# Another table of moved works in the plan of a causal attention and a two-layer product

## The chip, the cores and the metric

One Trainium2 chip, one core of it. The metric is the device time of one execution in microseconds; three executions give a median. A profiled execution is a run of its own, with its own time.

## The reference, cut to what matters

Four batches of twelve heads attend over 448 positions of 64 elements; the result, 1792 tokens of 768 elements, goes through two matrix products with an ELU between them. Everything is float32, except that the two weight matrices arrive as float64.

```python
scores = scale * np.matmul(q, k.transpose(0, 1, 3, 2))      # 4 x 12 x 448 x 448
scores = np.where(np.triu(ones, k=1), -1e9, scores)
attn = np.exp(scores - np.max(scores, axis=-1, keepdims=True))
attn = attn / (np.sum(attn, axis=-1, keepdims=True) + 1e-09)
x = np.matmul(attn, v)          # transposed and reshaped to 1792 x 768
h = x @ w_in                    # 768 x 2048
g = np.where(h > 0.0, h, np.exp(np.minimum(h, 0.0)) - 1.0)
return (g @ w_out)              # 2048 x 768
```

## The kernel before

**The work.** Positions are cut into four chunks of 112. Heads go in pairs (six of them), one head on each half of the 128 partitions. The first chunk of each pair is done first (`first_pair`, its q, k and v loaded at L500 and L505), then the second (`attention(False)`), then the third and fourth together (`attention(True)`, "joint"). Of a unit of attention TensorE (PE) makes the scores `sc` (L614, first chunk L515); VectorE (DVE) adds the mask and takes the row minimum of the negated scores `nm` (`softmax`, L419); ScalarE (ACT) takes the exponential and the row sums (L423); PE transposes the result (`tr`, L679), an engine copies it to SBUF (`at`: L683 on ACT, L684 on DVE), and PE multiplies it with v (`av`, L647, first chunk L453).

**The precision.** A float32 product is made as three matmuls (`three`, L817 to L819) of a rounded high part and a low part of each factor. The high part is a cast (`hi_lo`: L775 on ACT, or L776 on DVE) and the low part a subtraction on DVE (L778). The tile `whl` holds both parts of a weight tile, `qkhl` those of a joint pair's q and k (loaded as `qk`), `xh` and `xl` those of x. The first scores and the first hidden tiles use plain float32 (L515, L840).

**The weights.** A tile of `w_in` comes as 64-bit words (`load64`, L728). `convert` turns it into float32 in a chain of five steps that alternates between two engines: L736 on DVE, L740 on ACT, L741 on DVE, L744 on ACT (needs only the words, so it may be done early), and L747 on DVE. The converted tile is also stored (`kin`) and fetched again for the later tokens (`w<-kin`). Tiles of `w_out` are converted in the same way in the background, and four additions or subtractions (`add`, L783) mix four tiles for the products of the joint half.

**The ELU.** ACT makes `m` from a finished bank `hp` in two steps (L913, L914), and DVE makes `G` from both (L915).

**What sets the order.** Nothing is ordered by hand. All work is declared as 3130 works to a `Plan`, each with the engine that may do it, a rough cost, what it reads and writes, and a due time that is worked back from the PE work that needs it. A work with two ways, such as the casts of `hi_lo` and the copies `at`, may go to either engine. `draft` is a list scheduler: it walks through a model of time, and on the engine that is free earliest it places, among the ready works that can start within 0.12 us of each other, the one that is wanted first. The instructions are then issued in that order, so each engine executes its own row of works strictly in order, and an instruction that has to wait holds up all that stands behind it. All 449 DMAs are issued by SyncE (SP) in its row. The table that the change replaces enters in one line: the number of a work (in order of declaration) gives the microseconds by which its wanted time is moved, forward where positive.

```python
w.want = w.due - shift.get(w.n, 0.0)      # L218; shift is Plan.SOONER
```

**The stages.** PE's long stretches are: the first chunk with the first hidden tiles (0 to 30 us), the second chunk with the first half of the hidden layer (to about 120 us), the joint attention between products of the two halves (to about 375 us), and from there products alone.

Of the kernel before, what the change touches and what calls it, by code (L numbers as in the profile page):

```python
# [108 lines left out]
class Plan:  # L109
# [21 lines left out]
    def add(self, ways, reads=(), writes=(), due=None, size=0.0, hold=(), after=None):  # L131
# [24 lines left out]
        return w  # L156

    SOONER = {
# [30 lines left out]
    }  # L189

    def rank(self):
# [1038 lines left out]
```

## Time and profile before

| | us |
|---|---|
| three executions | 602.19, 604.09, 604.17 (median 604.09) |
| profiled execution, its time | 602.11 |
| its span in the profile | 600.3 |
| PE busy in the span | 588.2 (98%) |
| DVE busy | 517.3 (86%) |
| ACT busy | 440.6 (73%) |
| granted TensorE clock | 0.999 of full speed |

The span is what the profiler sees from the first to the last instruction; 1.8 us of the execution's own time lie around it. An engine's busy time is counted without the instructions that only wait, branch or issue DMAs.

### The profile page before, as it was taken

To read this page: it belongs to the slowest core of one execution; us is meant where nothing else is said; L and a number is where in the kernel's file an instruction comes from. 1 tells how busy PE (TensorE), PEld (TensorE's weight loads), DVE (VectorE), ACT (ScalarE), POOL (GpSimd) and SP (SyncE) were. 2 spreads that over 40 slices of the span, in tenths; PEclk is the share of its full clock that TensorE was granted. 3 is DMA by queue.
4 is the path that set the end of the run, shared out by engine and by line. 5 is a ranking of instruction groups with operands and counts; after the bars stand their busy time and mean duration, and the time that the engine had idled before them with its cause. 6 is when DMAs were issued, how large, how long until landed. Compare 5 with 4: busy or idle time off the path is not lost.

```text
span 600.3 us, 11631 instructions
## 1 busy us (share of the span) xinstructions
PE 588.2 (98%) x4086; PEld 518.2 (86%) x4086; DVE 517.3 (86%) x1212; ACT 440.6 (73%) x980; POOL 1.5 (0%) x12
## 2 busy tenths in 40 slices
PE   6999999999999999999999999999999999999997
PEld 5766888888788888888888889999999999999996
DVE  4889999999999999998999897699878999998511
ACT  6999989899899989887779766258747886574300
POOL 0000000000000000000000000000000000000000
PEclk9999999999999999999999999999999999999999
DMA  9999999988999999875456588996953334451111
GB/s 228 250 346 342 374 287 316 279 240 252 327 325 298 348 318 280 278 214 169 139 166 199 156 288 256 334 329 238 319 159 106 106 105 132 117 141 53 46 48 46
DMA packets 113610, 134.36 MB, mean 224 GB/s; under 512 B 42512, under 2 KB 86800, under 8 KB 113552
## 3 DMA queue, kind: packets, MB, share of 16 engines
q1 hardware_dynamic: 113552, 133.62, 72.2%
q8 instruction: 32, 0.52, 0.4%
q14 instruction: 26, 0.21, 0.1%
HBM read 101.45 MB, written 32.15 MB: 223 GB/s over the span
## 4 chain that ended last, share of the span: by engine, by line
PE 91%; DMA 2%; ACT 2%; SPq 2%; DVE 2%; issue 0%; ACTq 0%
PE op L817 12%; PE op L819 11%; PE op L818 11%; PE hp L817 11%; PE hp L819 10%; PE hp L818 10%; PE av L647 6%; PE tr L679 6%; PE sc L614 6%; PE hp L840 3%; DMA v<-in_v 1%; DMA w<-kin 1%; SPq L500 1%; PE av L453 1%; SPq L505 1%; ACT a L423 1%
## 5 line engine op out<-in xcount | busy, mean ns | idle before, releaser
L775 ACT ACTIVATE whl<-w 128x768 fp32r<-128x768 f32 x102 | 85.4, 842 | 75.5 <-PE op L819 41.2
L817 PE MATMUL op<-ph,whl 128*128 128x448 f32 (+1 forms) x338 | 126.4, 374 | 0.0
L819 PE MATMUL op<-ph,whl 128*128 128x448 f32 (+1 forms) x338 | 123.1, 364 | 0.0
L818 PE MATMUL op<-pl,whl 128*128 128x448 f32 (+1 forms) x338 | 123.1, 364 | 0.0
L778 DVE TENSOR_TENSOR whl<-w,whl 128x768 fp32r<-128x768 f32 x108 | 102.4, 953 | 14.4 <-ACT whl L775 14.0
L423 ACT ACTIVATE a<-a,nm 112x336 f32<-112x336 f32 (+3 forms) x192 | 98.0, 522 | 11.9 <-DVE nm L419 11.7
L419 DVE CUSTOM_DVE_ANT_0 a<-sc,mask 112x336 f32<-112x336 f32 (+3 forms) x192 | 74.7, 443 | 9.3 <-PE sc L515 7.4
L817 PEld LDWEIGHTS op<-ph,whl 128*128 128x128 f32 x338 | 63.5, 188 | 8.8 <-issue 3.8
L819 PEld LDWEIGHTS op<-ph,whl 128*128 128x128 f32 x338 | 63.5, 188 | 5.2
L818 PEld LDWEIGHTS op<-pl,whl 128*128 128x128 f32 x338 | 63.6, 188 | 4.5
L817 PE MATMUL hp<-xh,whl 128*128 128x448 f32 x168 | 65.6, 390 | 0.0
L819 PE MATMUL hp<-xh,whl 128*128 128x448 f32 x168 | 61.4, 366 | 0.0
L818 PE MATMUL hp<-xl,whl 128*128 128x448 f32 x168 | 61.4, 366 | 0.0
L818 PE MATMUL hp<-pl,whl 128*128 128x448 f32 x168 | 61.4, 365 | 0.0
L817 PE MATMUL hp<-ph,whl 128*128 128x448 f32 x168 | 61.4, 365 | 0.0
L819 PE MATMUL hp<-ph,whl 128*128 128x448 f32 x168 | 61.3, 365 | 0.0
L679 PE MATMUL tr<-ident,a 112*112 112x112 f32 x432 | 50.2, 259 | 0.5 <-DVE nm L419 0.4
L679 PEld LDWEIGHTS tr<-ident,a 112*112 112x112 f32 x432 | 45.1, 133 | 5.8 <-DVE nm L419 1.1
L683 ACT ACTIVATE at<-tr 112x448 f32<-112x448 f32 (+1 forms) x109 | 47.5, 497 | 1.5 <-PE tr L679 1.5
L647 PEld LDWEIGHTS av<-at,v 112*64 112x64 f32 x864 | 41.5, 137 | 5.5 <-issue 3.1
L647 PE MATMUL av<-at,v 112*64 112x112 f32 x864 | 45.4, 261 | 0.0
L913 ACT ACTIVATE m<-hp 128x448 f32<-128x448 f32 x56 | 30.2, 538 | 13.9 <-DVE hp L908 7.0
(96 smaller groups left out, 990.4 us busy)
## 6 DMA issues: line engine op xcount, KB each, us to landing
w<-kin SPq DMA_DIRECT2D x40, 384.0 KB, 5.4
w<-in_w_in SPq DMA_DIRECT2D x16, 768.0 KB, 9.1
w<-in_w_out SPq DMA_DIRECT2D x24, 512.0 KB, 6.3
w<-sout SPq DMA_DIRECT2D x32, 384.0 KB, 3.4
w<-kout SPq DMA_DIRECT2D x24, 384.0 KB, 3.2
qk<-in_qk SPq DMA_DIRECT2D x24, 336.0 KB, 5.3
kin<-w SPq DMA_DIRECT2D x16, 384.0 KB, 7.1
sout<-w SPq DMA_DIRECT2D x12, 512.0 KB, 5.6
```

What stands on the lines that cost most here:

```text
L419: plan.add(dve(n, lambda: nc.vector.tensor_tensor_reduce(out=a()[:, c], in0=sc()[:, c], in1=mask[:, S - n:], op0=ALU.add, op1=ALU.min, sca ...
L423: plan.add(act(n, lambda: nc.scalar.activation(a()[:, c], a()[:, c], AF.Exp, bias=nm()[:, x:x + 1], scale=-1.0, accum_out=su()[:, x:x + 1] ...
L614: nc.tensor.matmul(sc[half]()[:, lo:lo + n], s["q"](d, x), s["k"](d, y, n), start=i == 0, stop=i == len(s["split"]) - 1,)
L647: nc.tensor.matmul(av()[half_of(half), chunk(u % 4)], o["v"][1](half, i), at()[:, chunk(x)], start=i == 0, stop=i == chunks(u) - 1,)
L679: nc.tensor.transpose(tr()[:, chunk(x)], a[:, chunk(i)], ident)
L683: act(w, lambda: nc.scalar.activation(at()[:, :w], tr()[:, :w], AF.Copy)),
L775: act(n, lambda: nc.scalar.activation(h(), x(), AF.Copy), 0.09),
L778: sub = lambda eng: lambda: eng.tensor_tensor(out=l(), in0=x(), in1=f32(h()), op=ALU.subtract)
L817: nc.tensor.matmul(acc(), wh(k), xh(), start=first, stop=False, skip_group_check=more)
L818: nc.tensor.matmul(acc(), wh(k), xl(), start=False, stop=False, skip_group_check=more)
L819: nc.tensor.matmul(acc(), wl(k), xh(), start=False, stop=last, skip_group_check=more)
L913: plan.add(act(S, lambda: nc.scalar.activation(m(), h(), AF.Relu, scale=-1.0)), [h], [m])
```

## The change

The dictionary `Plan.SOONER` is replaced by another one, of 232 entries for 278. No work is added, removed or changed; the lines behind the table stand five lower in the changed file (L747 becomes L742, and so on). The core of the diff:

```diff
     SOONER = {
-        0: 284.3, 1: 284.4, 7: -8.8, 12: 1.9, 14: -2.2, 15: -3.8, 17: 0.4, 21: -14.5, 23: -45.2, 31: 0.6,
...
-        954: -56.2, 957: 27.7, 958: 15.4, 963: 11.1, 966: -8.3, 968: 88.8, 977: 58.1, 978: 7.9, 982: -7.1,
...
+        0: 668.6, 1: 670, 3: -4.9, 14: -1.3, 15: -10.9, 19: 4.7, 21: -8.6, 23: -35.1, 32: -1.1, 33: -17.8,
...
+        916: 5.3, 932: 23.9, 952: -11.7, 954: -11.8, 957: 32.2, 964: 338.3, 965: -159.4, 968: 198.3, 972: 12.7,
...
     }
```

PE executes the same 851 works as before, and its last 268 (from about 435 us) in the same order. Ahead of that many works change places on every engine. Some also change the engine: of the casts and copies, three `xh`, one `qkhl` and two `at` of 112x448 leave DVE for ACT on balance, and one `at` of 112x336 comes to DVE.

Three places show it. The first is SP's row at the start of the program. The loads of q, k and v there belong to the six first pairs; `w<-in_w_in` is the first 128-column tile of `w_in` (768 KB), the tile that the first conversion waits for. Before, it is the 13th instruction of the row:

```order
L500 DMA q_129<-in_qk 128x4x112
L500 DMA k_131<-in_qk 128x4x112
L728 DMA w_133<-in_w_in 128x1536
L505 DMA v_151<-in_v 112x4x64 x2
L505 DMA v_127<-in_v 112x4x64
L500 DMA q_182<-in_qk 128x4x112
L500 DMA k_189<-in_qk 128x4x112
L505 DMA v_195<-in_v 112x4x64 x2
```

The same place of SP's row after the change:

```order
L495 DMA q_127<-in_qk 128x4x112
L495 DMA k_129<-in_qk 128x4x112
L500 DMA v_131<-in_v 112x4x64
L500 DMA v_133<-in_v 112x4x64 x2
L500 DMA v_131<-in_v 112x4x64
L495 DMA k_164<-in_qk 128x4x112
L723 DMA w_182<-in_w_in 128x1536
L500 DMA v_189<-in_v 112x4x64
```

Four loads of v and one of k now stand ahead of the weight tile.

The second place is ACT's row at the end of the second chunk, 114 to 123 us in the trace of before. Before:

```order
L913 ACTIVATE m<-hp 128x448
L914 ACTIVATE m<-m 128x448
L423 ACTIVATE a,su<-a,nm 112x224 x6
L683 ACTIVATE at<-tr 112x448 x2
L423 ACTIVATE a,su<-a,nm 112x224 x2
L913 ACTIVATE m<-hp 128x448
L914 ACTIVATE m<-m 128x448
```

The same place after the change:

```order
L908 ACTIVATE m<-hp 128x448
L909 ACTIVATE m<-m 128x448
L770 ACTIVATE qkhl<-qk 128x672
L418 ACTIVATE a,su<-a,nm 112x224 x7
L678 ACTIVATE at<-tr 112x448 x2
L418 ACTIVATE a,su<-a,nm 112x224
L770 ACTIVATE xh<-xs 128x448
L908 ACTIVATE m<-hp 128x448
L909 ACTIVATE m<-m 128x448
```

A cast of `qkhl` stands ahead of the exponentials and a cast of `xh` behind them; both were on DVE.

The third place is DVE's row around the conversion and mixing of four background tiles (`w_2025`, `w_1941` or `w_1940`, and `w_2040`), 148 to 154 us in the trace of before. Before, from the second half of `w_2025`'s conversion to the minimum of the next joint softmax:

```order
L741 TENSOR_SCALAR w<-w 128x512
L915 SCALAR_TENSOR_TENSOR G<-m,hp 128x448
L741 TENSOR_SCALAR w<-w 128x512
L747 ISA w<-w_2025,w 128x1024
L783 TENSOR_TENSOR w_2025<-w 128x256
L783 TENSOR_TENSOR w_2025<-w_2025,w 128x256
L783 TENSOR_TENSOR w_2025<-w 128x256
L783 TENSOR_TENSOR w_2025<-w,w_2025 128x256
L736 TENSOR_SCALAR w<-w_2040 128x512
L747 ISA w<-w_1941,w 128x1024
L783 TENSOR_TENSOR w_1941<-w 128x256
L419 ISA a,nm<-sc,mask 112x336
```

The same place after the change:

```order
L742 ISA w<-w_1940,w 128x1024
L736 TENSOR_SCALAR w<-w 128x512
L742 ISA w<-w_2025,w 128x1024
L778 TENSOR_TENSOR w_2025<-w 128x256
L778 TENSOR_TENSOR w_2025<-w_2025,w 128x256
L778 TENSOR_TENSOR w_2025<-w 128x256
L778 TENSOR_TENSOR w_2025<-w,w_2025 128x256
L731 TENSOR_SCALAR w<-w_2040 128x512
L910 SCALAR_TENSOR_TENSOR G<-m,hp 128x448
L778 TENSOR_TENSOR w_1940<-w 128x256
L736 TENSOR_SCALAR w<-w 128x512
L414 ISA a,nm<-sc,mask 112x336
```

The conversion of one tile (L747, now L742) moves ahead of the chain of `w_2025`, and the step that makes `G` moves behind it, with an L741 (now L736) of the next tile, in front of the softmax.

## Rows read from the trace of the kernel before

**Rows 1.** The page's first part: busy us, share of the span and instructions.

```profile
PE 588.2 (98%) x4086; PEld 518.2 (86%) x4086; DVE 517.3 (86%) x1212; ACT 440.6 (73%) x980; POOL 1.5 (0%) x12
```

**Rows 2.** Windows: length, busy PE, PEld, DVE, ACT, POOL; clock, DMA share, GB/s.

```profile
0.00:30.00 30.00, 23.14 (x269) 19.05 (x270) 19.44 (x121) 24.34 (x87) 1.47 (x12) 1.00 0.99 239
30.00:120.00 90.00, 90.00 (x623) 72.09 (x622) 83.59 (x227) 82.56 (x196) 0.00 (x0) 1.00 1.02 324
120.00:175.00 55.00, 53.33 (x469) 45.61 (x468) 52.74 (x140) 48.67 (x114) 0.00 (x0) 1.00 0.92 283
175.00:435.00 260.00, 260.00 (x1929) 231.64 (x1928) 237.46 (x527) 200.27 (x443) 0.00 (x0) 1.00 0.81 256
```

**Rows 3.** PE's waits: what released it; total us, times, longest us.

```profile
PE av L453 <- DMA v<-in_v: 1.2, 1, 1.2
PE sc L614 <- DVE qkhl L778: 0.8, 1, 0.8
PE tr L679 <- DVE nm L419: 0.4, 1, 0.4
```

**Rows 4.** Timeline of the first weight tile: start, duration us, engine, operation, [idle before].

```profile
9.66 1.12 SPq L728 DMA_DIRECT2D w<-in_w_in  x1
18.12 0.56 DVE L736 TENSOR_SCALAR w<-w 128x768 f32<-128x768 f32 x1 [1.90 <-DMA w<-in_w_in]
20.67 0.85 ACT L740 ACTIVATE w<-w 128x768 f32<-128x768 f32 x1
24.24 0.96 DVE L747 CUSTOM_DVE_ANT_0 w<-w,w 128x1536 uint16<-128x1536 uint16 x1
25.87 1.39 PE L840 MATMUL hp<-xf,w 128*128 128x448 f32 x3
```

**Rows 5.** Chain that ended last, second-chunk scores: start, us, what.

```profile
51.78 1.93 PE sc L614 x16
...
69.08 1.70 PE sc L614 x16
```

**Rows 6.** Windows ahead of and in ACT's run of 140.67, columns as in Rows 2.

```profile
115.00:140.67 25.67, 25.67 (x242) 21.98 (x239) 24.34 (x75) 20.85 (x56) 0.00 (x0) 1.00 0.83 242
140.67:149.56 8.89, 8.89 (x74) 8.07 (x76) 8.62 (x24) 8.79 (x21) 0.00 (x0) 1.00 0.81 249
```

**Rows 7.** ACT's timeline: the two waits ahead of that run.

```profile
118.01 0.48 ACT L423 ACTIVATE a<-a,nm 112x224 f32<-112x224 f32 x1 [2.66 <-DVE nm L419]
...
140.67 0.85 ACT L775 ACTIVATE whl<-w 128x768 fp32r<-128x768 f32 x1 [0.65 <-PE sc L614]
```

**Rows 8.** Chain of waits behind that run, 149 to 164 us: start, us, what.

```profile
149.56 0.44 DVE w L741
...
152.63 0.61 DVE w L747
...
153.61 0.50 DVE a L419
...
156.70 7.33 DMA w<-kin
```

**Rows 9.** Groups by line and shape: count, busy us, mean ns, idle before.

```profile
L683 ACT ACTIVATE at<-tr 112x448 f32<-112x448 f32 x67 | 32.4, 536 | 1.2 <-PE tr L679 1.2
L915 DVE SCALAR_TENSOR_TENSOR G<-m,hp 128x448 f32<-128x448 f32 x40 | 24.5, 615 | 1.1 <-ACT m L914 0.9
L775 ACT ACTIVATE qkhl<-qk 128x672 fp32r<-128x672 f32 x21 | 16.0, 761 | 4.7 <-PE sc L614 1.9 <-issue 1.5 <-DMA qk<-in_qk 1.2
L684 DVE COPY at<-tr 112x448 f32<-112x448 f32 x5 | 3.0, 616 | 0.3 <-PE tr L679 0.3
L775 ACT ACTIVATE xh<-xs 128x448 fp32r<-128x448 f32 x3 | 1.7, 573 | 0.0
L776 DVE CAST qkhl<-qk 128x672 fp32r<-128x672 f32 x3 | 1.5, 505 | 0.0
L776 DVE CAST xh<-xs 128x448 fp32r<-128x448 f32 x3 | 1.2, 389 | 0.0
```

51 rows, old and new, of the table SOONER are left out of this document.

## The prediction

> **What bounds the kernel now.** The busy times come first: PE is busy for 588.2 of the span, DVE for 517.3 and ACT for 440.6 [rows 1], so PE sets the time and the other two only through its waits. The windows then say where PE has any: it is busy for 23.14 of the first 30 us, for all of 30 to 120, for 53.33 of the 55 us from 120 to 175, and for all of the 260 us from 175 to 435 [rows 2]. From 435 on its own order is unchanged. The change leaves PE's works as they are, so it can win only what PE loses now: the 1.2 us for a load of v in the start, since the waits for the very first loads stand ahead of everything that is moved, and 55 - 53.33 = 1.67 us in 120 to 175, of which 0.8 waits for the low part of `qkhl` from DVE and 0.4 for a row minimum from DVE [rows 3]. What it can lose has no such ceiling: DVE is busy for 52.74 of those 55 us and for 237.46 of the 260 that follow, and ACT for 82.56 of the 90 us from 30 to 120 [rows 2]. The granted clock is 1.00 in every window [rows 2], the upper level, and no term below rests on it.
>
> **The start.** The load of the first weight tile moves behind four more loads of v (112 KB each by their shape) and one more of k (224 KB), 672 KB in all. At the 239 GB/s of this window [rows 2] they take 672 x 1.024 / 239 = 2.9 us. Before, the load was issued at 9.66, and DVE's L736 waited for it until 18.12 [rows 4]; after, it lands at about 18.12 + 2.9 = 21.0. The five steps of the conversion hang on it. L736 takes 0.56, so ACT's L740 can start at 21.6, where it started at 20.67 [rows 4]: 0.9 us later, since ACT had other work until then. At the end of the chain L747 ended at 24.24 + 0.96 = 25.20 and PE's L840 began at 25.87 [rows 4], which is 0.67 us of slack. Against this the earlier v load takes the wait of 1.2 us away [rows 3], so PE would be ready for L840 at 25.87 - 1.2 = 24.7, and the weights at 25.20 + 0.9 = 26.1: PE starts it 0.2 us later than before. The bounds are -1.2 (the tile lands no later than ACT wants it) and +0.9 (all the delay reaches PE, because ACT's exponentials and copies stand behind the blocked L740). None of a gain lasts: the second chunk's first scores at 51.78 took 1.93 where the same 16 matmuls took 1.70 at 69.08 [rows 5], so PE already waits 0.23 inside them, I take it for their load, and with the DMA engines full from 30 to 120 (share 1.02 [rows 2]) that load comes no earlier when PE does. The same 0.23 swallows a delay of 0.2. I take 0.0 for the start.
>
> **What moves from DVE to ACT.** Over the whole kernel three casts of `xh`, one of `qkhl` and two copies of 112x448 leave DVE, and one copy of 112x336 comes to it. By the means of [rows 9] DVE gives away 3 x 0.389 + 0.505 + 2 x 0.616 = 2.9 us, and takes back at most 0.62 (the 448 copy is the larger): 2.3 off. ACT takes 3 x 0.573 + 0.761 + 2 x 0.536 = 3.6, less at most 0.54: 3.0 on. All but one `xh` lie in 115 to 158 us, so there DVE is 1.9 us lighter and ACT 2.4 us heavier. ACT has room: from 115 to 140.67 it is busy for 20.85 of 25.67 us [rows 6], 4.8 free, 2.66 of them in one wait for DVE's minima at 118.01 [rows 7]. The `qkhl` cast (0.76) now stands exactly ahead of those exponentials, and the other 1.6 us have the 2.2 that remain. Should its load come late, the cast still costs nothing until 2.66 - 0.76 = 1.9 us of delay. So ACT's next run begins at 140.67 as before, when PE's scores release it [rows 7].
>
> **The chain behind that run.** From 140.67 to 149.56 ACT is full (8.79 of 8.89 [rows 6]); its last L740 releases DVE's L741 at 149.56, from there L747, the additions and another L747 (0.61 at 152.63) lead to the joint softmax at 153.61, and that to PE's transposes and, over a released buffer, to a fetch of weights that takes 7.33 us from 156.70 [rows 8]. On ACT, one L744 comes into the run and one exponential leaves it, which I take as equal. On DVE, the L747 of 0.61 moves ahead, where DVE waits for ACT anyway, while `G` (L915, 0.615 [rows 9]) and an L741 (0.44 [rows 8]) now stand between the additions and the softmax: 0.615 + 0.44 - 0.61 = +0.45, the softmax at 154.06 and its transposes on PE 0.45 later. What PE waits for next is the low part of `qkhl` (the 0.8 of [rows 3]). Ahead of it DVE loses one copy of 112x336 (under 0.62 [rows 9]) to ACT, which gives the 0.45 back; so the scores that now wait start when they did, and the transposes' delay lies inside a wait that PE had. The 0.4 for a row minimum [rows 3] stays too: DVE's row in front of that minimum keeps its length. I take 0.0 here, between -1.67, where all of PE's idle time goes, and +2.3 (worked out below).
>
> A rule of the Trainium skill speaks for more: "Perfetto Trace Analysis", section "Optimizing Scalar/DVE Operations", says that where DVE is saturated, work that either engine can do may well be moved to the scalar engine. DVE is close to that here, 52.74 of 55 us [rows 2], but the engine that would take the work is itself full for the 8.8 us ahead of the wait; by the rule the time would be that of the first rival.
>
> **175 to 435 us, and the end.** PE never idles there, so nothing can be won. Many works change places on all engines, and a place that slips costs what one wait of that sort costs now, 0.4 to 0.8 [rows 3]. Two such places would be +1.6. DVE has 260 - 237.46 = 22.5 us free and ACT 59.7 [rows 2], and no row points at a place that is short, so I take 0.0, with 0 to +1.6 as bounds. The end, from 435, is 0.0.
>
> **The sum.** 0.0 + 0.0 + 0.0: the profiled execution's 602.11 would stay 602.1. It lies 1.98 below the median of 604.09, to which I refer the forecast: **604.1 us**. A measurement of this kernel can tell about 0.5%, 3.0 us, from no change: below 601.1 is faster, above 607.1 slower.
>
> **Rivals.** *DVE's relief counts.* The 1.9 us that DVE loses ahead of 158 us lie on a nearly full engine, whose waits PE feels. If ACT delivers its casts on time, the minima and low parts come earlier by more than the waits, and PE's 1.67 us go: 602.4. With the 1.2 of the v load as well, if the cap at 51.78 doesn't hold, 604.1 - 2.9 = 601.2, and if the 0.23 inside the scores there goes too, 601.0. For it speaks that DVE is the releaser of 1.2 of the 1.67 [rows 3]; against it that the order puts two steps in front of the very softmax, and that the chain passes through ACT. Chance 0.25.
>
> *ACT's run starts late.* If the 2.4 us don't find their gaps (the free time lies between exponentials that DVE feeds), the casts push ACT's row back, and the run at 140.67 has no room in it. PE's own pace absorbs the first 0.65 there [rows 7]; from that point on each microsecond goes through L740 and L741 to the softmax. At worst 2.4 - 0.65 = 1.75 on ACT and the 0.45 of DVE's new order, +2.2, and with the fetch of 156.70 pushed behind others about 0.1 more, +2.3: 606.4. If the 0.65 doesn't absorb anything, 604.1 + 2.4 + 0.45 = 607.0, and slips behind 175 add to it. For it speaks how full ACT is in this stretch, against it the 4.8 us free ahead. This is the case that ends slower. Chance 0.22.
>
> *The weight tile is missed.* ACT holds 0.9 us of exponentials and copies back behind the blocked L740 and the delay doesn't drown in the wait at 51.78: 604.1 + 0.9 = 605.0. For it speaks that ACT is at 24.34 of 30 us and then at 82.56 of 90 [rows 2]. Chance 0.10.
>
> *Nothing is felt*, as forecast, 603.3 to 604.9: 0.38. The remaining 0.05 is for something that the rows don't show, at either side.
>
> **How the numbers follow.** The likeliest is 604.1. The range reaches from 600.9 (the first rival with its three parts, less 0.1) to 607.2 (the second at its worst, plus 0.2 of the start); beyond it lie slips behind 175 on top of the second rival, about 0.08, and a chance remainder of 0.05. Faster by over 0.5%: a little over half of the first rival's chance would need all its parts, which I put at 0.10, and 0.05 for the spread of the three executions (602.19 to 604.17), together 0.15. Slower by over 0.5%: half of the second rival, 0.11, and 0.05 for the same spread and the unknown, 0.16. Within 0.5%: 0.69.
>
> **What would show it.** In the changed profile: the wait for v in the first 30 us is gone, ACT's L735 (L740 before) on the first tile starts near 21.6, and L835 near 26.1; the second chunk's first scores again end at about 53.7. From 115 to 141 ACT is busier by about 2.4 us, and its run of exponentials behind starts between 140 and 141.3. Scores still wait 0.8 for the low part of a `qkhl`, and PE is busy for 53.3 of 120 to 175. From 175 to 435 PE stays at 260. The forecast is wrong if PE's busy time in 120 to 175 is above 54.5 or below 52.5, if the scores at 51.78 move by more than 0.3, or if a wait turns up behind 175.

## The result, and the profile after

The changed kernel takes 608.98 us (median; 607.46 to 610.21), the kernel before 603.5 beside it: a ratio of 1.0101, with an interval of 1.0083 to 1.0119. It is 5.5 us slower, outside the forecast range of 600.9 to 607.2. The profiled execution took 609.91 us, with a span of 608.1; the one of before had 602.11 and 600.3, so in the traces 7.8 us have to be found. That is more than the 5.5 of the medians, because the profiled execution of before was faster than most of its others, and that of the changed kernel slower than most.

The page's first part for the changed kernel, to be held against [rows 1]:

```profile
PE 592.4 (97%) x4086; PEld 521.2 (86%) x4086; DVE 514.7 (85%) x1206; ACT 443.2 (73%) x986; POOL 1.5 (0%) x12
```

DVE is 2.6 us lighter and ACT 2.6 heavier, as the casts and copies should make them. But PE is 4.2 us busier with the same 4086 matmuls, and its span has grown by 7.8. The windows of the changed kernel (columns as in [rows 2]) say where:

```profile
0.00:30.00 30.00, 21.41 (x241) 18.34 (x242) 17.02 (x102) 21.95 (x76) 1.48 (x12) 0.89 1.02 244
30.00:120.00 90.00, 90.00 (x625) 71.31 (x626) 83.00 (x229) 84.46 (x200) 0.00 (x0) 1.00 0.98 309
120.00:175.00 55.00, 53.56 (x461) 45.54 (x463) 50.73 (x143) 48.94 (x121) 0.00 (x0) 1.00 0.93 278
175.00:435.00 260.00, 257.94 (x1926) 229.03 (x1923) 232.41 (x522) 197.69 (x438) 0.00 (x0) 0.99 0.81 251
```

Two stretches differ from [rows 2]: in the first 30 us PE is busy for 21.41 at a clock of 0.89, where it was busy for 23.14 at 1.00, and in the last it is idle for 2.06, where it was never idle. PE's waits in the changed kernel name them (what released it; total us, times, longest):

```profile
PE rb L530 <- DVE rr L424: 2.8, 1, 2.8
PE sc L609 <- ACT at L678: 2.1, 1, 2.1
PE sc L609 <- DVE qkhl L773: 0.8, 1, 0.8
PE tr L674 <- DVE nm L414: 0.4, 1, 0.4
```

The last two are those of [rows 3]. The wait for v is gone; the first two are new. To place the loss, the same work is looked up in both traces. PE's timeline of the kernel before (start, duration, engine, line, operation), two rows ahead of and behind the second new wait:

```profile
175.02 0.45 PE L817 MATMUL hp<-xh,whl 128*128 128x448 f32 x1
...
182.53 0.47 PE L817 MATMUL hp<-xh,whl 128*128 128x448 f32 x1
```

And of the changed kernel, the first hidden tile of [rows 4] and the same two:

```profile
29.82 1.02 PE L835 MATMUL hp<-xf,w 128*128 128x448 f32 x2
...
178.80 0.45 PE L812 MATMUL hp<-xh,whl 128*128 128x448 f32 x1
...
188.82 0.74 PE L812 MATMUL hp<-xh,whl 128*128 128x448 f32 x1
```

The changed kernel is 29.82 - 25.87 = 3.95 us behind at the first hidden tile, 178.80 - 175.02 = 3.78 at 175 us, 188.82 - 182.53 = 6.29 behind the second wait and 7.8 at the end. So 4 us go in the start, nothing in the 145 us that follow, and 4 us between 180 and 200; from there to the end the distance stays. The 7.8 us are 4.2 of longer busy time and 3.6 of idle time; the two new waits of 2.8 and 2.1, less the 1.2 for v, make 3.7.

**The first loss.** DVE's timeline in the changed kernel, 17 to 22 us ([..] is the idle time before, and what ended it):

```profile
17.29 0.20 DVE L424 RECIPROCAL rr<-rr 112x8 f32<-112x8 f32 x1
...
20.63 0.56 DVE L731 TENSOR_SCALAR w<-w 128x768 f32<-128x768 f32 x1 [1.98 <-DMA w<-in_w_in]
21.10 0.61 DVE L516 TENSOR_REDUCE su<-a 112x4 f32<-112x448 f32 x1
21.82 0.17 DVE L423 TENSOR_SCALAR rr<-su 112x8 f32<-112x8 f32 x1
22.03 0.20 DVE L424 RECIPROCAL rr<-rr 112x8 f32<-112x8 f32 x1
```

And PE's timeline there:

```profile
18.52 1.04 PE L510 MATMUL sc<-k,q 64*112 64x112 f32 x16
22.37 1.76 PE L530 MATMUL rb<-ident,rr 112*64 112x112 f32 x16 [2.82 <-DVE rr L424]
...
25.36 1.76 PE L530 MATMUL rb<-ident,rr 112*64 112x112 f32 x16
```

`rb` spreads the reciprocals `rr` of a pair's row sums over the partitions. The rr that PE waits for are the fourth pair's, and they stand on DVE behind L731, which waits for the late weight tile. The rr of the third pair were ready at 17.29 + 0.20 = 17.5, but PE has them later in its row now. The kernel before shows what is new in this. There the fourth pair's rr and the `rb` that uses them were:

```profile
22.15 0.19 DVE L429 RECIPROCAL rr<-rr 112x8 f32<-112x8 f32 x1
23.50 0.94 PE L535 MATMUL rb<-ident,rr 112*64 112x112 f32 x16
```

So these rr were ready at 22.34 before and are ready at 22.23 now: they are no later (22.34 to 22.88 in the four traces of the kernel before and its variants, 21.21 to 22.44 in the ten of the changed kernel and its variants). PE asks for them earlier, right behind scores that end at 18.52 + 1.04 = 19.56.

Behind the wait the 16 matmuls of `rb` take 1.76 us, where they took 0.97 at 15.79. The windows show why (the third number from the right is the granted clock, in parts of the upper level):

```profile
20.00:25.00 5.00, 2.63 (x23) 2.38 (x24) 4.23 (x23) 4.39 (x11) 0.00 (x0) 0.64 1.15 259
25.00:30.00 5.00, 5.00 (x52) 4.03 (x51) 2.58 (x5) 3.28 (x11) 0.00 (x0) 0.68 1.05 296
```

A mean of 0.64 and 0.68 over five microseconds means that the clock stood at its lower level, 1.2 GHz, for the larger part of them; over the 1.76 us of the first `rb` alone, 22.37 to 24.13, the trace gives 0.50. It fell within PE's wait of 2.82 us: the first microsecond of it has 1.00, its end 0.50. The Trainium skill says in "TensorE: Matmul & The Clock Gate", section "Part 1: The HAM clock gate", that PE's clock is lowered when PE has been idle. That agrees with this trace; traces below show waits of 2.2 us behind which the clock did not fall.

**The second loss.** ACT's timeline in the changed kernel, 183 to 188 us:

```profile
183.38 0.85 ACT L770 ACTIVATE whl<-w 128x768 fp32r<-128x768 f32 x1 [2.82 <-DMA sout<-w]
...
187.03 1.29 ACT L678 ACTIVATE at<-tr 112x336 f32<-112x336 f32 x3
```

And PE's, around the joint scores that wait for the copy `at`:

```profile
185.05 0.40 PE L609 MATMUL sc<-qkhl 64*112 64x336 f32 x1
187.51 1.38 PE L609 MATMUL sc<-qkhl 64*112 64x336 f32 x11 [2.06 <-ACT at L678]
```

In the kernel before, this cast `whl` (L775 there) did not wait:

```profile
176.61 0.83 ACT L775 ACTIVATE whl<-w 128x768 fp32r<-128x768 f32 x1
```

A cast `whl` waits on ACT until a store of mixed weights (`sout`) has landed, though the cast reads nothing of that store. The store reads a word tile `w64`; tiles `w64`, `whl` and `qkhl` share eight places in SBUF, and in the changed kernel this `whl` was given the place of that `w64`. The built programs' addresses show it: in the kernel before it has the place of an earlier `whl`, which PE had finished with. In order behind the cast stand the exponentials and the copies `at`, and PE's next scores need the bank that the copy empties. Here too the clock falls, as a window of the changed kernel shows:

```profile
188.80:192.20 3.40, 3.40 (x10) 3.03 (x10) 3.40 (x13) 3.34 (x7) 0.00 (x0) 0.52 1.05 326
```

The next twelve matmuls of `hp` take from 188.82 to 192.82, where nine took 184.46 - 182.53 = 1.93 in the kernel before. The instructions behind the twelve and behind the nine are:

```profile
192.82 1.50 PE L674 MATMUL tr<-ident,a 112*112 112x112 f32 x14
...
184.46 0.93 PE L679 MATMUL tr<-ident,a 112*112 112x112 f32 x8
```

### The profile page after: what moved, and what is told of

It is laid out like the page before. It is cut to its first block, busy times and chain, and to the rows that moved or that the text cites. A ratio compares the mean times of both kernels' runs of the same rounds, so it can differ in the third digit from the quotient of the medians.

```text
span 608.1 us, 11651 instructions
## 1 busy us (share of the span) xinstructions
PE 592.4 (97%) x4086; PEld 521.2 (86%) x4086; DVE 514.7 (85%) x1206; ACT 443.2 (73%) x986; POOL 1.5 (0%) x12
## 4 chain that ended last, share of the span: by engine, by line
PE 89%; DMA 6%; SPq 2%; ACT 1%; DVE 1%; issue 0%; DVEq 0%; ACTq 0%
PE op L812 12%; PE op L813 11%; PE op L814 11%; PE hp L812 11%; PE hp L813 10%; PE hp L814 10%; PE av L642 6%; PE sc L609 6%; PE tr L674 6%; PE hp L835 3%; DMA w<-in_w_out 2%; DMA sout<-w 1%; DMA w<-in_w_in 1%; DMA w<-kin 1%; SPq L495 1%; SPq L500 1%
```

## The experiments

All of them take the changed kernel or the kernel before. Most move single works in the finished order, so that all other rows stay as they are; three add matmuls on PE instead or as well. Where works are moved, the lines added behind `draft` are the same each time; `MOVED` names a work and the work in front of which it is put:

```diff
         order = self.draft(self.SOONER)
         assert order, "no work can start"
+        for n, m in self.MOVED:
+            o = next(x for x in order if x[0].n == n)
+            order.remove(o)
+            order.insert(next(i for i, x in enumerate(order) if x[0].n == m), o)
```

The theory before these runs is that two waits with the slow clock behind them are the whole loss: the first made by the late weight tile, by DVE's row behind it and by PE's row together, the second by the place in SBUF alone. The rivals: one of the three parts makes the first wait by itself; the clock has no share; the load that ACT took over is behind the second.

| run | median us | ratio to before (interval) | first hidden tile | granted clock, all executions |
|---|---|---|---|---|
| changed kernel again | 608.49 | 1.0087 (1.0065 to 1.0109) | 29.12 | 0.992 to 0.994 |
| load early | 607.61 | 1.0101 (1.0052 to 1.0151) | 26.48 | 0.994 to 1.000 |
| reciprocals first on DVE | 607.59 | 1.0083 (1.0053 to 1.0113) | 26.34 | 0.992 to 0.997 |
| `rb` exchanged on PE | 606.02 | 1.0081 (1.0058 to 1.0105) | 24.65 | 0.994 to 1.000 |
| 44 matmuls in the wait | 611.39 | 1.0160 (1.0140 to 1.0179) | 32.96 | 0.997 to 1.000 |
| 14 matmuls in the wait | 605.62 | 1.0060 (1.0040 to 1.0080) | 27.71 | 0.997 to 1.000 |
| place exchanged | 605.22 | 1.0055 (1.0034 to 1.0076) | 28.10 | 0.994 to 1.000 |
| `rb` and place | 602.74 | 1.0004 (0.9988 to 1.0019) | 24.69 | 0.999 to 1.000 |
| `rb` and 20 matmuls at 182 | 607.98 | 1.0095 (1.0066 to 1.0125) | 24.90 | 0.999 to 1.000 |
| before, load late | 603.10 | 1.0014 (0.9998 to 1.0029) | 25.66 | 0.997 to 1.000 |
| before, `rb` early | 603.19 | 1.0014 (1.0000 to 1.0029) | 28.70 | 0.997 to 1.000 |
| before, place exchanged | 603.76 | 1.0026 (1.0008 to 1.0043) | 25.78 | 0.999 to 1.000 |

The first hidden tile is the start of the first matmul of `hp<-xf,w` in the profiled execution, 25.87 in [rows 4]. Each ratio is to the kernel before run beside it, whose medians were 601.8 to 602.8. The variants of the changed kernel spread over 2 to 7 us from one execution to the next, the kernel before over 2 to 4, so small differences between the medians prove nothing. A trace shows one execution.

### The changed kernel again

> The changed kernel itself once more, on the chip of the other runs, for a number beside theirs. Theory (two waits, each with the slow clock behind it): about 1% over the kernel before, granted clock near 0.993 in every run, since both waits are above 2 us each time. Rival (the first six runs were a chip's own): the loss is under 0.5% here.

The loss is there again, and all four executions have a clock of 0.992 to 0.994. In the trace PE's waits are 2.2 (rr) and 2.3 us (at), and the first hidden tile starts at 29.12.

### The load early

> The changed kernel with one move: the load of the first weight tile goes back from 18th to 13th place in SP's row, ahead of the four loads of v and the load of k; everything else stands as in the changed kernel. Theory (the late tile): DVE's first L736 waits for the tile until 20.6 us, the reciprocals rr of the fourth pair stand behind it, and PE's rb of that pair waits 2.8 us for them. With the tile landing near 18.1, rr comes at about 21 instead of 22.2, PE's wait falls from 2.8 to at most 1.5 us, and the slow stretch behind it shrinks with it: 3 to 4 us off the changed kernel's time. Against it: the loads of v come later again, up to 1.2 us of wait. Rival (PE's order alone): rb was moved forward in PE's row, and rr is bound by ACT's exponentials as much as by the tile, so PE still waits over 2 us there: within 1 us of the changed kernel.

```diff
+    MOVED = (
+        (252, 76),
+    )
```

In the trace the wait for rr falls to 1.3 us, the clock stays at 1.00, and the first hidden tile starts at 26.48, 3.3 us earlier than in the changed kernel. Of these 3.3, only 0.7 are the earlier `rb` (21.70 for 22.37); the rest is the clock, which stayed up in this execution. So the late tile has a small share. One load of v stays ahead of the tile here, as in the kernel before. The median shows little of it (607.61, between 604.58 and 611.22): in the traced execution, the fastest, the clock is 1.000, and in the two slowest 0.994.

### Reciprocals first on DVE

> The changed kernel with one move on DVE: the first step of the first weight tile's conversion (L731, which waits for the load) stands behind the reciprocals of the fourth pair instead of ahead of them; SP, ACT and PE stand as in the changed kernel, so the tile is as late and rb as far forward. Theory (what is queued behind the waiting instruction): the reciprocals wait only for ACT's exponentials, which end at 20.4 us, and come at about 21.0 instead of 22.2; PE's wait for them falls from 2.8 to about 1.5 us and the slow stretch behind it goes or shrinks; 2.5 to 3.5 us off the changed kernel's time. The weight tile's conversion starts 0.4 us later, within the slack of PE's first hidden tile. Rival (ACT sets rr, not DVE's row): the wait stays above 2.3 us, and the time within 1 us.

```diff
+    MOVED = (
+        (257, 152), (258, 260),
+    )
```

DVE's timeline of this kernel, 20 to 22 us:

```profile
20.29 0.62 DVE L524 TENSOR_REDUCE su<-a 112x4 f32<-112x448 f32 x1 [1.84 <-ACT a L426]
21.01 0.17 DVE L431 TENSOR_SCALAR rr<-su 112x8 f32<-112x8 f32 x1
21.22 0.20 DVE L432 RECIPROCAL rr<-rr 112x8 f32<-112x8 f32 x1
```

Freed from the tile, the sum waits for ACT's exponentials instead, and rr come 0.8 us earlier (21.22 for 22.03). PE, which was earlier too, still waits 2.2 us. The wait of 2.2 lies nearer to the rival's 2.3 than to the theory's 1.5: ACT sets rr nearly as late as the tile does, and DVE's row is a small part. The traced execution shows something else: after a wait of 2.2 us its clock is 1.00 from 20 to 30 us, where the changed kernel's was 0.61 and 0.71 after the same 2.2 in its second trace. The windows from 20 to 25 us, of this kernel and of that second trace:

```profile
20.00:25.00 5.00, 3.43 (x52) 2.91 (x52) 4.20 (x23) 3.80 (x9) 0.00 (x0) 1.00 1.16 282
...
20.00:25.00 5.00, 3.60 (x30) 3.07 (x32) 4.62 (x23) 4.41 (x11) 0.00 (x0) 0.61 1.12 240
```

Such a wait makes the clock fall in some executions and not in others.

### `rb` exchanged on PE

> The changed kernel with one move on PE: the rb of the third pair, whose reciprocals were ready at 17.5 us, changes places with the rb of the fourth pair, for which PE waited 2.8 us; DVE, ACT and SP stand as in the changed kernel, so the weight tile is as late as there. Theory (PE's order): the wait of 2.8 goes to 0.7 or less, other short waits of up to 1.4 us for a copy of at come up, no slow stretch follows; 2.5 to 4 us off the changed kernel's time. Rival (the late tile): PE runs into the same late DVE a little further on, for xf and the first weight tile, and the time falls by under 1 us.

```diff
+    MOVED = (
+        (106, 143), (143, 102),
+    )
```

PE's timeline of this kernel, the scores and both `rb`, without a wait for rr:

```profile
18.12 1.04 PE L518 MATMUL sc<-k,q 64*112 64x112 f32 x16
19.09 0.99 PE L538 MATMUL rb<-ident,rr 112*64 112x112 f32 x16
...
21.39 0.99 PE L538 MATMUL rb<-ident,rr 112*64 112x112 f32 x16
...
24.65 1.02 PE L843 MATMUL hp<-xf,w 128*128 128x448 f32 x2
```

The tile's load stands where the changed kernel has it, though in this trace the tile came 1.7 us earlier than in that kernel's first (DVE took it up at 18.91). The first hidden tile starts 5.2 us earlier than in the changed kernel and 1.2 us earlier than in the kernel before. None of the three traces with this exchange has a wait for rr, so PE's order is the part without which the first loss isn't there. The second wait remains, 2.2 us in this trace, here without a fall of the clock. By the ratios the time fell by 0.4 to 1.2 us, less than expected: the other executions were up to 5.8 us above the traced one, most of them with a clock of 0.994 to 0.997.

### 44 and 14 matmuls in the wait

> The changed kernel with 44 more matmuls of 112x112 ahead of the rb of the fourth pair, whose results are overwritten: they fill about 2.6 of the 2.8 us for which PE waits there, and delay nothing else. Theory (the clock): a large part of the loss in the start is the slow stretch behind the wait (granted clock 0.64 and 0.68 in 20 to 25 and 25 to 30 us); with PE busy the clock stays at its upper level there, and the time falls by 2 to 3 us although PE's work grows by 2.6. Rival (the wait itself): the clock has nothing to do with it, the work behind is slow for want of its operands; the time stays within 0.5 us.

```diff
         def spread():
+            for _ in range(44 * (p == 3)):
+                nc.tensor.matmul(r()[:D, :CP], ident[:, :D], mask[:, :CP], start=True, stop=True)
             for b in range(B):
```

That was mis-sized: the 44 took 8.55 us, so the kernel became slower. They show the price of one, 0.19 us. In the trace each of them stands as two instructions, as each matmul of `rb` does, so 14 are 28 there. With 14:

> The changed kernel with 14 more matmuls of 112x112 ahead of the rb of the fourth pair. A first try with 44 showed that each takes 0.19 us, so they took 8.55 us for a wait of 2.8; 14 take 2.7. Theory (the clock): the stretch from that rb to the first hidden tile, 7.45 us in the changed kernel, takes 5 us, and the time falls by 2 to 3 us. Rival (the wait itself): no more than 0.5 us is won.

PE's timeline of the kernel with 14, and its two windows:

```profile
20.26 2.80 PE L528 MATMUL rb<-mask,ident 112*64 112x112 f32 x27
22.80 0.31 PE L532 MATMUL rb<-ident,rr 112*64 112x112 f32 x1
...
27.71 1.02 PE L837 MATMUL hp<-xf,w 128*128 128x448 f32 x2
```

```profile
20.00:25.00 5.00, 5.00 (x68) 4.60 (x66) 4.02 (x23) 4.39 (x12) 0.00 (x0) 1.00 1.14 258
25.00:30.00 5.00, 5.00 (x60) 3.47 (x57) 4.90 (x21) 4.79 (x20) 0.00 (x0) 1.00 0.98 263
```

From the start of `rb` to the first hidden tile it is 27.71 - 22.80 = 4.91 us, for 29.82 - 22.37 = 7.45 in the changed kernel. The work is the same and rr were as late (ready at 22.44); PE was only kept busy. Where the clock stayed up without a fill, with the load early and with the reciprocals first, the same stretch took 4.78 and 4.77. So the slow clock is 2.5 of the 4 us of the first loss. The ratio is 1.0060, where the changed kernel has 1.0101 and 1.0087: work added on PE for nothing made the kernel about 2 us faster (1.6 by the one, 2.5 by the other).

### The place exchanged

> The changed kernel with two tiles exchanging their places in SBUF at 183 us: the cast whl on ACT that waited 2.8 us for the store sout takes the place that a finished whl left, and the load of the next word tile takes the place that the store reads. Every engine's row stands as in the changed kernel. Theory (the place): ACT's cast starts at 180.6 instead of 183.4, the copies at behind it come 2 us earlier, PE's wait of 2.1 us at 185 goes, and the clock stays up: 3 to 4 us off the changed kernel's time; the load waits 0.7 us more on SP, which nobody feels. Rival (ACT is late anyway, by the work that it took over): the wait moves to the next releaser, and the time falls by under 1 us.

```diff
+    MOVED = (
+        (1143, 1117), (1206, 1117), (1180, 1117),
+    )
```

The three are loads on SP; putting them ahead of the cast 1117 in the list changes no engine's row, only who is given which place. ACT's timeline of this kernel, where no wait stands before the cast:

```profile
180.94 0.83 ACT L778 ACTIVATE whl<-w 128x768 fp32r<-128x768 f32 x1
```

The store landed at 183.79 in this trace, and nobody waited for it; PE's wait for `at` is gone. The ratio of 1.0055 is 2 to 3 us below the changed kernel's two; the first wait is still there, 2.0 us in this trace with the clock at 0.77 and 0.89 in the windows from 20 to 30 us. In the nine traces in which the cast has the store's place, it starts 0.02 to 0.08 us after the store's landing, and ACT is idle for 1.1 to 3.6 us before it. That includes the opposite exchange:

> The kernel before with two tiles exchanging their places in SBUF, the other way round than in the run on the changed kernel: the cast whl at 176.6 us takes the place that the store sout of a mixed word tile still reads, and the load of the next word tile takes the place of a finished whl. Every engine's row stands as in the kernel before. Theory (the place alone makes the second wait): the cast starts with the landing of that store, which lay at 178.3 in the kernel before, ACT loses 1.7 to 2.5 us, its copies at come as much later, and PE's joint scores at 181 us wait 1 to 2 us for them: 1 to 2 us slower, up to 4 where the clock falls behind the wait. Rival (the change's other moves, and ACT's new load, are needed): within 0.7 us of the kernel before.

```diff
+    MOVED = (
+        (1172, 1117), (1143, 1117), (1180, 1117),
+    )
```

ACT's timeline of the kernel before with that exchange:

```profile
178.35 0.85 ACT L783 ACTIVATE whl<-w 128x768 fp32r<-128x768 f32 x1 [1.10 <-DMA sout<-w]
```

The median is 1.5 us above the kernel before, with the clock at 0.999 or more throughout. So the place alone makes ACT's wait; the work that ACT took over isn't needed for it. It does not show PE's wait in full: in this trace the scores behind it run for 1.80 us where they ran for 1.32, so PE lost 0.5 us there, while 1.0 us had gone in the first 60 us, which the exchange doesn't touch. ACT's wait is also the shortest of the nine. Whether ACT's new load makes it longer in the changed kernel was not tested.

### Both

> The changed kernel with two moves together: the rb of the third and fourth pair change places on PE, and the cast whl at 183 us takes the place of a finished whl. Theory (two separate waits, each with the slow clock behind it, are the whole loss): both waits go, PE comes out of the start 1.3 us earlier than in the kernel before, as it did with the first move alone, and keeps that lead to the end: 600.5 us where the kernel before has 601.8, that is 0 to 0.3% below the kernel before. Rival (there are more causes behind 185 us, ACT's and DVE's new load): 2 us or more above the kernel before.

The windows of this kernel:

```profile
0.00:30.00 30.00, 24.73 (x274) 19.57 (x276) 20.11 (x122) 24.57 (x89) 1.47 (x12) 1.00 1.07 265
...
120.00:175.00 55.00, 54.07 (x471) 45.95 (x470) 51.98 (x137) 50.05 (x119) 0.00 (x0) 1.00 0.92 281
175.00:435.00 260.00, 260.00 (x1923) 231.36 (x1922) 234.17 (x520) 199.15 (x440) 0.00 (x0) 1.00 0.81 254
```

Two exchanges bring the changed kernel to 1.0004 of the kernel before, -0.7 to +1.1 us by the interval: the whole loss, as far as these runs can tell. The lead that was expected is in the trace but not in the median. All twelve executions have a clock of 0.999 or more. Everything else in the table of 232 entries, hundreds of moved works and the casts on the other engine, together costs nothing and brings nothing that could be measured. No variant was measurably faster than the kernel before. Singly the two exchanges take less off the ratio, 0.1 to 0.2% and 0.3 to 0.5%, than together, 0.8 to 1.0%; the intervals are too wide to say whether the two losses only add up.

### The parts alone in the kernel before

> The kernel before with one part of the change alone: the load of the first weight tile stands behind three more loads of v and one of k (560 KB). Everything else stands as in the kernel before. Theory (the late tile is enough): DVE's L736 waits until 20.5 instead of 18.1, the reciprocals of the third and fourth pair behind it come 2.4 us later, and PE's two rb wait about 0.3 and 1.2 us: 1.5 us slower than before, or up to 4 with a slow stretch behind. Rival (it needs PE's order as well): within 0.7 us of the kernel before.

```diff
+    MOVED = (
+        (252, 185), (186, 252),
+    )
```

The median is 0.8 us up (0 to 1.7 by the interval), nearer to the rival. In the trace the wait for v is gone, PE waits 1.2 us for DVE instead, and the first hidden tile starts at 25.66. But the tile came only 0.45 us later than in the kernel before there (DVE took it up at 18.57), so the trace is a weak test of a late tile.

> The kernel before with another part of the change alone: on PE the rb of the fourth pair stands right behind the scores of the fifth, ahead of the transposes and the rb of the third pair. Everything else stands as in the kernel before. Theory (it needs the late tile as well): rb waits for its reciprocals until 22.35 instead of starting at 23.5, PE loses about 1 us there and gets part of it back in the waits that follow; 0 to 1 us slower. Rival (PE's order is enough): 2.5 us or more slower, with a slow stretch behind.

```diff
+    MOVED = (
+        (143, 135),
+    )
```

The median is 0.9 us up, as the theory has it. But in the traced execution PE waits 2.06 us for rr, its clock falls (0.75 and 0.90 in the two windows from 20 to 30 us) and the first hidden tile starts at 28.70. Two of the ten executions have a clock of 0.997, the others 0.999 or 1.000. So PE's order alone makes the wait, with the tile taken up at 16.72, and in some executions the slow clock behind it. The changed kernel's ten executions were all at 0.992 to 0.994. The late tile may make the difference (waits of 2.8 and 2.2 us there, 2.06 here), but that isn't shown: with the load early, two of the four executions were at 0.994 too.

### A fill for the second wait

> The changed kernel with the rb of the third and fourth pair exchanged (as in the run that did that alone) and with 10 more matmuls of 112x112 at 180 to 185 us, ahead of the joint scores that wait 2.2 us for ACT's copy at; their results are overwritten, and at about 0.2 us each they fill the wait. The place of the cast whl stays as in the changed kernel, so the wait itself is still there. The run without the fill had a median of 606.0 at granted clocks of 0.994 to 1.000, with 603.7 in an execution at 0.999. Theory (the spread is the clock behind this wait, which falls in some executions and not in others): the clock is 0.999 or more in all executions, and the time lies at 603.5 to 604.5 in each, 1.5 to 2 us under the median without the fill. Rival (the clock falls elsewhere): clocks of 0.994 to 0.997 are still among the executions, and the median stays within 0.7 us.

```diff
                 def fn(s=s, sc=sc, n=n, lo=lo):
+                    for _ in range(10 * (plan.done[-1].n == 1097)):
+                        nc.tensor.matmul(sc[0]()[:, :CP], ident, mask[:, :CP], start=True, stop=True)
```

This one failed in its making: the work has two units, so 20 matmuls were added, and the second ten stood behind the wait and cost 2.2 us; in the trace the first ten took 2.1 and a wait of 1.1 remained. It still says something: the clock was 0.999 or more in all four executions, and they spread from 606.68 to 609.47 all the same. The kernel before, at 0.999 or more as well, spread from 601.41 to 603.77 beside it. So some 2 to 3 us of spread are not the clock; four of the variants with executions at 0.994 or less spread over 4 to 7. What the rest is was not settled; the landing of the store, 5.3 to 8.1 us from its issue in the traces, varies by as much, and in this trace alone a second cast on ACT, a `qkhl`, waits 2.5 us for the next store `sout`.

## Why the prediction was wrong

**The start, the failed step.** The sizes were nearly right. I counted four loads of v ahead of the tile, but one of them stood ahead of it before as well, since the tile was the 14th of SP's row and not the 13th: 560 KB, 2.4 us. L731 ran at 20.63 (forecast 21.0) and ACT's L735 at 21.22 (forecast 21.6), and the wait for v went. The weights were ready at 25.60 (forecast 26.1). But the first hidden tile was forecast for 26.1 and came at 29.82. The step that failed is "PE would be ready for L840 at 25.87 - 1.2 = 24.7": it took PE's row for that of before with one wait gone. PE's row had changed. The `rb` of the fourth pair had come forward past ready work, PE waited 2.82 us for reciprocals that were no later than before, and the clock fell. With the two `rb` exchanged PE did start the tile at 24.65. I followed the late tile along its own chain and along ACT's row, asked neither what stands behind the waiting L731 on DVE (the sum and the reciprocals of the fourth pair) nor when PE would want it, and never compared PE's row in the start. The bound of +0.9, and the rival "the weight tile is missed" with its 605.0, named the right stretch at a quarter of its price, and by another path: ACT's row, not PE's.

**The clock, the mis-sized term.** "No term below rests on it" was wrong in kind. Waits on PE were priced at their length. A wait of 2 to 3 us costs its length and, where the clock falls, the slow stretch behind it: 2.5 us in the start, by the run with 14 matmuls, and about 12 x (0.333 - 0.214) = 1.4 us behind the second wait, from the twelve and the nine matmuls shown above. Together that is 3.9 of the 4.2 us by which PE was busier.

**The cap at 51.78** did not hold as put. With `rb` and place exchanged PE was 1.2 us ahead at the first hidden tile, and its span ended at 599.7 for 600.3. Nor did its 0.23 swallow anything: in the changed kernel these scores start at 55.72, about 4 us later, one of the signs that the forecast had named. The time shows no gain (1.0004), so a lead doesn't matter for the sum, but the reading that a load holds PE there was a guess from one row.

**DVE's relief and the chain of 140 to 175 us** came out as forecast: 3.95 us behind at the first hidden tile, 3.78 at 175 us, so nothing won or lost there. ACT's run starts at 144.46, 3.8 after 140.67, released by PE's scores as before: the rival "ACT's run starts late" didn't happen. With both waits taken away PE was busy for 54.07 of the 55 us, 0.7 more than in [rows 2], without an effect on the time that could be measured. The rule of the Trainium skill ("Perfetto Trace Analysis", "Optimizing Scalar/DVE Operations") brought nothing here: DVE was 2.6 us lighter, and no run shows a gain from it; the moved casts and copies were not tested by themselves.

**175 to 435 us, the second failed step.** I put 0.0 to +1.6 because PE was never idle there and no row pointed at a short place. The loss was 4 us at one place that no comparison of the engines' rows can show, because it lies in which tile has which place. What would have shown it is what the cast waits for in the built program: one DMA, and not the one that loads its operand. Its price is the wait of 2.06 us and the 1.4 above, beyond the upper bound.

**The chances.** 0.69 for "within 0.5%" came from adding small terms at places that I had looked at. Several hundred works moved at places that I had not, with PE at 98%, and for what the rows don't show the text held 0.05.

## What to carry to other kernels

Where a table or a scheduler reorders a kernel whose bottleneck engine never idles, the bottleneck's own row comes first: for each instruction that moves forward there, ask when its operand is ready and what now stands ahead of that operand on the engine that makes it. Here a new wait on PE of 2 to 3 us cost its length where the clock stayed up, and up to 1.9 times its length where it fell (2.82 + 2.5 us in the start); price it so, and weigh whether PE can be given other ready work there (the exchange of two `rb` did it). And when tiles of several kinds share a pool, a new order also hands out new places: look in the built program for an instruction that waits for something that it doesn't read.

## What the runs showed of the hardware

- The clock's answer to a wait is not the same from one execution to the next: 2.2 us of waiting left it at its upper level in one kernel's trace (reciprocals first, 1.00 from 20 to 25 us) and brought it down in another's (the changed kernel's second trace, 0.61), with the wait at the same place.
- Useless matmuls can pay: 14 of 0.19 us each in a wait of 2.8 us made the changed kernel about 2 us faster, since the 7.45 us of work behind the wait took 4.91.
- The 16 matmul instructions of `rb` took 0.99 us at the upper level (reciprocals first, 21.57 us) and 1.76 at the lower (0.50 in the changed kernel from 22.37 to 24.13 us), less than twice as long.
